# Reading the early token lists before the first expert's weights, and moving GpSimd's drains, in a fused attention and mixture-of-experts kernel

## The chip, the cores and the metric

The kernel runs on one core of one Trainium2 chip. The metric is the device time of one execution in microseconds (us). Three executions of the kernel before took 772.63, 769.27 and 769.30 us; their median is 769.3 us.

The engines are called here as the profile calls them: PE (TensorE, matrix products; PEld are its weight loads), DVE (VectorE), ACT (ScalarE), POOL (GpSimd) and SP (SyncE, which here issues only DMAs and register loads). Each works through its own instructions strictly in program order, so an instruction that waits holds up all that stands behind it on its engine.

## The reference

```python
def _attn_ref(q, k, v):                     # (8 batches, 12 heads, 448 tokens, 64)
    scores = scale * np.matmul(q, k.transpose(0, 1, 3, 2)) - np.log(S)
    attn = 1.0 / (1.0 + np.exp(-scores))    # sigmoid, no sum over a row
    return np.matmul(attn, v)

def _moe_ref(x, w_gate, w_output_gate, w1, w2):   # x: 3584 tokens x 768, 8 experts, hidden 1024
    logits = x @ w_gate
    e_idx = np.argmax(logits, axis=1)             # each token goes to one expert
    probs = softmax(logits);  gate_w = probs[arange(N), e_idx]
    eom = 1.0 / (1.0 + np.exp(-(x @ w_output_gate)))
    for e in range(E):
        h = np.maximum(x[mask] @ w1[e], 0.0)
        out[mask] = gate_w * eom[mask, e] * (h @ w2[e])
```

All of it is float32. The softmax is cut to one line above.

## The kernel before

**Attention.** 48 head pairs (8 batches x 6) are worked off in 24 groups of two, each group in 7 units, so in 168 units. The code counts units backwards: unit -168 is the first and -1 the last. One unit is `scores(u)` on PE (L823), one sigmoid of 128x896 on ACT (L825) and `values(u - 2)` on PE (L832). The scores of unit u go into one of two PSUM buffers, so they wait for the sigmoid of unit u - 2. DVE adds and transposes a head pair's result (L835 to L846); after six pairs SP writes the batch to DRAM (`x_dram`, L848). SP also loads the keys, queries and values of group g + 2 (L815, 1344 KB each) when group g runs.

**Routing.** When a batch is complete, `gates` and the generator `route` give every token its expert and its place in that expert's list. `route` has four steps, called logits, counts, places and rows, which the attention loop calls at fixed units. The last one scatters the tokens' records into the DRAM table `lst` with four indirect DMAs on POOL (L325); they write the same table, and each waits until the one before has landed. For batch 6 (the last but one) two row gathers for the second slot stand behind each scatter.

**Slots.** The experts' work is cut into slots of 256 tokens. The first three, the early slots, take only tokens of batches 0 to 5, so that they can be prepared while attention still runs; `table` (L327 on) computes on DVE which expert and which place in the list each has. To prepare a slot, SP loads its list of 256 records (`load_list`, L458), DVE transposes it and POOL spreads it into index tiles (`spread_lists`, L463), POOL gathers the rows of x with eight indirect DMAs (`gather`, L507), DVE turns them (`turn_x`, L566), and ACT and DVE split them into a rounded high part and a low rest (`split_x`). The expert's weights are loaded by SP (`load_w`, L528) and split in the same way. In a slot PE does layer 1 (L588, L589) and layer 2 (L613 to L615); while it does, DVE, ACT, POOL and SP prepare the next two slots.

**What is done during attention** is in `unit(u)` (L896): the table in units -31 to -29, the first expert's six weight rows from -28 on (L910) with their splits two units apart from -22 on (L912), the first slot's list at -21 (L914), its spreading and gather at -18, the other two early lists at -18 and their spreading at -11, the second-layer weights from -9 on, `turn_x` at -8 and `split_x` at -6, -5 and -4.

**Lists of the later slots.** The generator `side()` (L945) is stepped from the early slots' loops. It finishes the routing, computes the late table on DVE (`table_late`) and then loads the later lists in blocks of 32 rows by indirect DMAs on POOL (`load_rows`, L498); the first block is transposed on DVE right after `turn_x` of the second slot.

**Drains.** `nc.gpsimd.drain()` lets POOL go on only when its earlier work is over. The kernel before has one in the fourth slot (L661) and one at the start of each slot behind it (L643, and L703 and L741 in the slots of other shapes).

Names in the rows: `lst` the table of records, `lxs` and `lts` the spread indices, `rounded` the split weights and inputs of layer 1, `plain` their float32 raw form (and the gathered rows), `w2h`/`w2l` the split second-layer weights, `gl` the sums of layer 1, `hb` the later lists.

Of the kernel before, what the change touches and what calls it, by code (L numbers as in the profile page):

```python
# [9 lines left out]
F32 = mybir.dt.float32  # L10
# [11 lines left out]
NPAIR = H // 2  # L22
# [11 lines left out]
EARLY_BATCH = 5  # L34
ROWS_E = (EARLY_BATCH + 1) * S
EARLY = -(-(ROWS_E - E * (TS - 1)) // TS)
# [7 lines left out]
GT = 32  # L44
LGR = LATE_N // 4
KT = REST // TS
READY = (EARLY_BATCH + 1) * NPAIR + 4
OOB = 1 << 20
LROWS = (E * CAP + TS) // 128
ROUNDED = (12 * DF + 12 * TS) * 4  # L50
# [8 lines left out]
class Kernel:  # L59
# [19 lines left out]
    def memory(self):  # L79
        self.rounded = self.pool("rounded").tile([128, ROUNDED // 4], F32R, name="rounded")  # L80
        self.plain = self.pool("plain").tile([128, PLAIN // 4], F32, name="plain")
        ps = self.pool("psum", space=PSUM).tile([128, 8, 512], F32, name="ps")
        self.ps_s = [ps[:, 0:2], ps[:, 2:4]]
        self.ps_third = ps[:, 6:8]
        self.ps_o = [[ps[:, 4], ps[:, 5]], [ps[:, 6], ps[:, 7]]]
        self.mm_ps, self.mm_late = ps[:, 5], ps[:, 7]
        self.gp = ps[:, 6, 0:QT]
        self.psx = [ps[:, i].rearrange("p (d t) -> p d t", d=2) for i in (6, 7)]
        self.psh = [ps[:, i] for i in (0, 1, 2, 4, 5)]
        self.psy = [ps[:, i, 0:384] for i in (4, 5, 3, 6)]  # L90
        self.rot = {}

        c = self.carve
        w = c(0, 3, 2, 2, DF)
        self.w1s = [[w[:, d // 2, a, d % 2] for d in range(6)] for a in range(2)]
        self.w1p = [[w[:, k, a] for k in range(3)] for a in range(2)]
        self.xc = c(12 * DF * 4, 6, 2, TS)
        self.xs = [self.xc[:, :, i] for i in range(2)]

        self.w1r = c(0, 6, DF, dt=F32)  # L100
        o = 6 * DF * 4
        self.xg = c(o, 8, Q4, dt=F32)
        self.xT = c(o + XG, 6, TS, dt=F32)
        o += 2 * XG
        self.w2r = c(o, 8, DM, dt=F32)
        self.li = c(o, LROWS, 6, dt=F32)
        self.lr_e = [c(o + LROWS * 24 + i * 768, 192, dt=F32, parts=32) for i in range(2)]
        self.tmp_early = o + 4096
        self.step = c(o + 8192, B, 4, dt=F32)
        self.tokf = c(o + 8192 + 16 * B, NCH, 4, dt=F32)  # L110
# [135 lines left out]
    def init_list(self):  # L246
        nc = self.nc
        nc.gpsimd.memset(self.li, 0.0)
        for w in range(1, 4):
            nc.gpsimd.memset(self.li[:, :, w:w + 1], float(w * S))  # L250
        nc.gpsimd.memset(self.li[:, :, 4:5], float(OOB))
        nc.gpsimd.dma_start(self.lst.rearrange("(p r) w -> p r w", p=128), self.li)
        for raw in self.lr_e:
            nc.gpsimd.memset(raw, 0.0)

    def route_tiles(self):
        rp = self.pool("route")
# [197 lines left out]
        self.rot[key] = i + 1  # L455
        return tiles[i % len(tiles)]

    def load_list(self, tab, k, raw, g):  # L458
        o = self.nc.values_load(tab[0:1, 1, k:k + 1], engines=[ET.SP], min_val=0, max_val=E * CAP)
        n = raw.shape[0]  # L460
        self.nc.sync.dma_start(raw, self.lst[bass.ds(o, 32 * n), :].rearrange("(g t) w -> g (t w)", t=32))
# [177 lines left out]
    def slot(self, m, side=None, hint=None):  # L639
        tab, k = (self.tab_e, m + 1) if m + 1 < EARLY else (self.tab_l, m + 1 - EARLY)  # L640
        nx = self.load_slot(tab, k, self.lists(m + 1))
        if m > EARLY:
            self.nc.gpsimd.drain()  # L643
        self.split_w2(0)
        for f in range(8):
            if m > EARLY and f == 6:
                self.finish()
            self.layer1(f, m == 0 and f == 0)
            if f == 0 and hint is not None:
                hint()  # L650
            if f:
                self.high_low(f - 1)
            if m == 0 and f < 7:
                next(side)
            if f in (1, 3, 5):
                self.split_w2(f // 2 + 1)
            if m and side is not None and f < 7:
                next(side, None)
        self.high_low(7)
        if m == EARLY:  # L660
            self.nc.gpsimd.drain()  # L661
        self.load_w2(nx)
        self.high_w1(0)
        self.turn_x(nx)
        if m == 0:
            next(side, None)
        if m == 1:
            next(side, None)
        self.gather(self.lists(m + 2), ROWS_E if m + 2 < EARLY else NT)
        for k in range(3):  # L670
            self.split_x(nx, k)
        self.low_w1(0)
        for i, (t, n) in enumerate(((0, 0), (0, 1), (1, 0), (1, 1))):
            if i == 3 and m >= EARLY:
                self.layer2_due(self.lists(m), 1)
            else:
                ps = self.psy[(0, 1, 3)[i] if m >= EARLY else (4 * m + i) % 3]
                self.layer2(self.lists(m), t, n, self.ys[t], ps)
            if i < 2:
                self.split_w1(i + 1)  # L680
            if side is not None and i > 0:
                for _ in range(3 if m == 0 and i == 1 else 1):
                    next(side, None)
# [110 lines left out]
    def attention(self, pool, rows):  # L794
        nc = self.nc
        N = B * NPAIR
        NG = N // G
# [19 lines left out]
        def scores(u):  # L817
            g, i = divmod(u, U)
            kg = kq[g % 3]
            ps = self.ps_third if u == 2 else self.take("s", self.ps_s)  # L820
            for j, h in corners:
                e, o = (h, 384) if i == 3 else (i // 4, 128 * (i % 4) + 64 * h)
                nc.tensor.matmul(ps[half[h], j, 0:S], kg[half[j], e, 1, o:o + 64], kg[half[j], e, 0],  # L823
                                 start=True, stop=True)
            nc.scalar.activation(at[u % 4], ps[:, :, 0:S], AF.Sigmoid, bias=self.bias_s, scale=1.0 / math.sqrt(D))  # L825
# [27 lines left out]
        def routing(at):  # L853
            if routes and want[0] == at:
                want[0] = next(routes[0])
                if want[0] is None:
                    routes.pop(0)
# [17 lines left out]
        for u in range(U * NG + LAG):  # L875
            g, i = divmod(u, U)
            self.unit(u - U * NG)
            if i == 1:
                routing("places")
            if u < U * NG:  # L880
                scores(u)
            if u >= LAG:
                values(u - LAG)
            if i == 3 and g and g % 3 == 0:
                gates(g // 3 - 1)
                routing("logits")
            if i == 1 and 0 < g < NG - 2:
                load(g + 2)
            for r, name in ((0, "counts"), (3, "rows")):
                if i == r and (name != "rows" or g != NG - 2):  # L890
                    routing(name)
        self.layer1_mm(0)
        gates(B - 1)
        return routes[-1]

    def unit(self, u):  # L896
        if u == -161:
            self.row_words()
        if u == -154:
            self.init_list()  # L900
        if u == -31:
            self.tgen = self.table()
        if -31 <= u < -28:
            next(self.tgen)
        if u == -28:
            self.s0 = dict(self.lists(0), **self.slot_regs(self.tab_e, 0))
        s = self.s0 if u >= -28 else None
        for d in range(6):
            if u == -28 + d:
                self.load_w(s, self.w1, self.w1r, [d], 1)  # L910
            if u == -22 + 2 * d:
                self.split_w1_row(d)  # L912
        if u == -21:
            self.load_list(self.tab_e, 0, self.lr_e[0][0:8], 8)  # L914
        if u == -18:
            self.spread_lists(self.lr_e[0], self.lts[:, 0:1], self.lxs[:, 0:1])
            self.gather(s, ROWS_E)
            for k in range(1, EARLY):
                self.load_list(self.tab_e, k, self.lr_e[1][8 * k - 8:8 * k], 8)
        if u == -11:  # L920
            self.spread_lists(self.lr_e[1], self.lts[:, 1:EARLY], self.lxs[:, 1:EARLY])
        for k in range(4):
            if u == -9 + 2 * k:
                self.nc.vector.memset(self.w2r[0:1, 2 * k, 0:1], 0.0)
                self.load_w(s, self.w2, self.w2r, [2 * k])
        if u == -8:
            self.turn_x(s)
        for k, at in enumerate((-6, -5, -4)):
            if u == at:
                self.split_x(s, k)  # L930

    def build(self, phases="abc"):
        tc, nc = self.tc, self.nc
# [13 lines left out]
        def side():  # L947
# [12 lines left out]
            for _ in self.table_late():  # L960
                yield
            at = lambda a, n: (self.lts[:, EARLY + a:EARLY + a + n], self.lxs[:, EARLY + a:EARLY + a + n])
            self.load_rows(0)
            yield
            for i in (1, 3):
# [101 lines left out]
```

## Time and profile before

| | before |
|---|---|
| median of 3 executions | 769.3 us (769.27 to 772.63) |
| the profiled execution's own time | 772.41 us |
| its span, first to last instruction | 770.7 us |
| PE busy | 758.6 us (98%) |
| ACT busy, DVE busy | 488.5 us (63%), 486.5 us (63%) |
| POOL busy | 349.3 us (45%) |
| DMA | 145.22 MB, mean 188 GB/s |

The profile comes from one execution, the 772.41 us one. Its span leaves out 1.7 us around the first and the last instruction. An engine's busy time counts the time in which it has an instruction under way. PE's idle time is 12.1 us in all: 1.3 us at the start, some 7 us behind its last product at the end, and the rest in short waits. Attention ends, and the first slot begins, at about 273 us.

### The profile page before, as it was taken

The numbers are of one execution on the slowest core, as the hardware profiler recorded it, in microseconds if no ns is written. First come the engines' busy times: TensorE is split into PE (matmuls) and PEld (weight loads), VectorE is DVE, ScalarE is ACT, GpSimd is POOL, SyncE is SP. The second block draws the span as 40 slices with busy tenths as digits, with TensorE's granted clock in tenths as the row PEclk, the third lists the DMA queues.
The fourth block names the chain that finished last, engine by engine and source line by source line (L and its number), as shares of the span: only waits on it lengthen the run. The fifth ranks groups of instructions, "written<-read, shape, count | busy, mean of one in ns | idle before, by whom it ended". The sixth has DMA issues, their size and how long they took to land. (4 is left out here: it accounts for less than half of the span.)

```text
span 770.7 us, 15634 instructions
## 1 busy us (share of the span) xinstructions
PE 758.6 (98%) x5971; PEld 563.7 (73%) x5971; DVE 486.5 (63%) x800; ACT 488.5 (63%) x662; POOL 349.3 (45%) x472
## 2 busy tenths in 40 slices
PE   9999999999999999999999999999999999999996
PEld 4344444444444379799999989999998999889785
DVE  3343443434356668878686676768586685877887
ACT  5666666666668756566574655747465574675686
POOL 4021303122132657777785667264362724524622
PEclk9999999999999999999999999999999999999999
DMA  7353454435349450147667497611146846397692
GB/s 265 136 217 126 169 207 146 163 129 217 131 174 348 156 166 17 43 175 251 239 205 256 162 344 269 201 57 37 47 174 210 307 161 218 123 337 251 228 411 67
DMA packets 37904, 145.22 MB, mean 188 GB/s; under 512 B 5671, under 2 KB 7951, under 8 KB 33840
## 3 DMA queue, kind: packets, MB, share of 16 engines
q1 hardware_dynamic: 27984, 119.56, 43.6%
q0 software_dynamic: 9824, 24.46, 9.6%
q8 instruction: 50, 0.82, 0.4%
q14 instruction: 46, 0.38, 0.1%
HBM read 152.61 MB, written 23.05 MB: 228 GB/s over the span
## 5 line engine op out<-in xcount | busy, mean ns | idle before, releaser
L588 PE MATMUL ps<-rounded 128*128 128x512 f32 (+1 forms) x672 | 226.0, 386 | 2.0 <-DVE gl L597 1.4
L825 ACT ACTIVATE a<-ps,bias_s 128x896 f32<-128x896 f32 x168 | 169.0, 1007 | 89.6 <-PE ps L823 89.5
L510 POOL DMA_INDIRECT plain<-x_dram,lxs x122 | 180.8, 1482 | 65.2 <-issue 31.9
L589 PE MATMUL ps<-rounded 128*128 128x256 f32 (+1 forms) x672 | 183.9, 274 | 0.0
L823 PE MATMUL ps<-kqv 64*64 64x448 f32 x1344 | 157.9, 542 | 1.1 <-ACT a L825 1.1
L832 PE MATMUL ps<-a,kqv 64*64 64x448 f32 x1344 | 155.9, 536 | 0.0
L545 DVE TENSOR_TENSOR w2l<-plain,w2h 128x1536 fp32r<-128x1536 f32 x60 | 105.2, 1756 | 64.8 <-ACT w2h L544 64.8
L613 PE MATMUL ps<-w2h,h 128*128 128x384 f32 x432 | 144.8, 335 | 0.0
L588 PEld LDWEIGHTS ps<-rounded 128*128 128x128 f32 x672 | 125.9, 187 | 25.6 <-DVE gl L597 2.3
L615 PE MATMUL ps<-w2h,h 128*128 128x384 f32 x432 | 144.4, 334 | 0.0
L614 PE MATMUL ps<-w2l,h 128*128 128x384 f32 x432 | 144.4, 334 | 0.0
L589 PEld LDWEIGHTS ps<-rounded 128*128 128x128 f32 x672 | 127.3, 189 | 0.0
L832 PEld LDWEIGHTS ps<-a,kqv 64*64 64x64 f32 x1344 | 50.9, 133 | 75.4 <-issue 74.2
L551 DVE TENSOR_TENSOR rounded<-plain,rounded 128x2048 fp32r<-128x2048 f32 x46 | 103.4, 2283 | 1.9 <-ACT rounded L548 1.9
L823 PEld LDWEIGHTS ps<-kqv 64*64 64x64 f32 x1344 | 49.7, 134 | 72.7 <-issue 68.2
L596 ACT COPY gl<-ps 128x256 f32<-128x256 f32 (+1 forms) x112 | 40.3, 360 | 95.2 <-PE ps L589 89.3
L544 ACT CAST w2h<-plain 128x1536 fp32r<-128x1536 f32 x60 | 88.2, 1472 | 16.7 <-PE ps L863 5.0
L548 ACT CAST rounded<-plain 128x2048 fp32r<-128x2048 f32 x46 | 87.2, 1902 | 0.0
L613 PEld LDWEIGHTS ps<-w2h,h 128*128 128x128 f32 x432 | 81.1, 188 | 2.3 <-issue 1.8
L614 PEld LDWEIGHTS ps<-w2l,h 128*128 128x128 f32 x432 | 81.1, 188 | 0.1
L615 PEld LDWEIGHTS ps<-w2h,h 128*128 128x128 f32 x432 | 81.1, 188 | 0.0
L635 POOL DMA_INDIRECT out<-y,due x11 | 18.3, 1660 | 113.3 <-ACT gl L596 92.7
(211 smaller groups left out, 699.8 us busy)
## 6 DMA issues: line engine op xcount, KB each, us to landing
plain<-w SPq DMA_DIRECT2D x68, 768.0 KB
plain<-w SPq DMA_DIRECT2D x48, 1024.0 KB
kqv<-kqv SPq DMA_DIRECT2D x23, 1344.0 KB
x_dram<-xt SPq DMA_DIRECT2D x8, 1344.0 KB
plain<-w SPq DMA_DIRECT2D x6, 512.0 KB
plain<-x_dram,lxs POOLq DMA_INDIRECT x122, 4.1
kqv<-kqv SPq DMA_DIRECT2D x2, 448.0 KB
lst<-plain POOLq DMA_DIRECT2D x1, 726.0 KB, 8.3
```

Of the source, the lines that this page charges most:

```text
L510: self.nc.gpsimd.indirect_dma_start(out=s["xg"][:, g], out_offset=None, in_=x4, in_offset=bass.IndirectOffsetOnAxis(ap=s["lx"][:, g:g + 1] ...
L544: self.nc.scalar.copy(hi, raw)
L545: self.nc.vector.tensor_tensor(lo, raw, r32(hi), ALU.subtract)
L551: self.nc.vector.tensor_tensor(self.w1p[1][k], self.w1r[:, 2 * k:2 * k + 2], r32(self.w1p[0][k]), ALU.subtract)
L588: nc.tensor.matmul(out, wh[d][:, c], both, start=(d == 0), stop=False)
L589: nc.tensor.matmul(ps[:, 0:n], wl[d][:, c], self.xc[:, d, 0, 0:n], start=False, stop=(d == 5))
L613: nc.tensor.matmul(ps, hh[:, f, tk], wh, start=(f == 0), stop=False)
L614: nc.tensor.matmul(ps, hh[:, f, tk], wl, start=False, stop=False)
L615: nc.tensor.matmul(ps, hl[:, f, tk], wh, start=False, stop=(f == 7))
L823: nc.tensor.matmul(ps[half[h], j, 0:S], kg[half[j], e, 1, o:o + 64], kg[half[j], e, 0], start=True, stop=True)
L825: nc.scalar.activation(at[u % 4], ps[:, :, 0:S], AF.Sigmoid, bias=self.bias_s, scale=1.0 / math.sqrt(D))
L832: nc.tensor.matmul(self.ps_o[e][h][half[j], 0:S], v[half[h], 6 if i == 3 else 3 * e + c, j], a[half[h], j], start=(i in ((0, 3 if h else 4 ...
```

## The change

The three early lists are loaded together at unit -27, ahead of the first expert's weights on SP's queue, and are spread at once at -21; the second spreading at -11 is gone. The weight rows are loaded from -25 instead of -28, and split from -18 instead of -22. Batch 6's rows step is called at the first unit of the last group instead of its fourth. One drain is put at unit -40, one ahead of the first block of the later lists; the one in the fourth slot is taken out.

```diff
@@ memory, init_list
-        self.lr_e = [c(o + LROWS * 24 + i * 768, 192, dt=F32, parts=32) for i in range(2)]
+        self.lr_e = c(o + LROWS * 24, 192, dt=F32, parts=32)
...
-        for raw in self.lr_e:
-            nc.gpsimd.memset(raw, 0.0)
+        nc.gpsimd.memset(self.lr_e, 0.0)
@@ slot
         self.high_low(7)
-        if m == EARLY:
-            self.nc.gpsimd.drain()
         self.load_w2(nx)
@@ attention
             for r, name in ((0, "counts"), (3, "rows")):
-                if i == r and (name != "rows" or g != NG - 2):
+                if i == (0 if g == NG - 1 else r) and (name != "rows" or g != NG - 2):
                     routing(name)
@@ unit
     def unit(self, u):
+        if u == -40:
+            self.nc.gpsimd.drain()
...
         for d in range(6):
-            if u == -28 + d:
+            if u == -25 + d:
                 self.load_w(s, self.w1, self.w1r, [d], 1)
-            if u == -22 + 2 * d:
+            if u == -18 + 2 * d:
                 self.split_w1_row(d)
+        if u == -27:
+            for k in range(EARLY):
+                self.load_list(self.tab_e, k, self.lr_e[8 * k:8 * k + 8])
         if u == -21:
-            self.load_list(self.tab_e, 0, self.lr_e[0][0:8], 8)
-        if u == -18:
-            self.spread_lists(self.lr_e[0], self.lts[:, 0:1], self.lxs[:, 0:1])
+            self.spread_lists(self.lr_e, self.lts[:, 0:EARLY], self.lxs[:, 0:EARLY])
             self.gather(s, ROWS_E)
-            for k in range(1, EARLY):
-                self.load_list(self.tab_e, k, self.lr_e[1][8 * k - 8:8 * k], 8)
-        if u == -11:
-            self.spread_lists(self.lr_e[1], self.lts[:, 1:EARLY], self.lxs[:, 1:EARLY])
@@ side
             at = lambda a, n: (self.lts[:, EARLY + a:EARLY + a + n], self.lxs[:, EARLY + a:EARLY + a + n])
+            nc.gpsimd.drain()
             self.load_rows(0)
```

SP's queue before, from the last two weight rows (`plain<-w`) on: the first list (`plain<-lst`), then batch 6's write of x and the load of the last group's keys, queries and values. A name in brackets is a semaphore that the instruction waits for; DMASW is a DMA of POOL, DMAHW one of SP.

```order
45 L531 DMA plain<-w 128x1024 [waits DMAHW4_49]
46 L531 ISA
47 L531 DMA plain<-w 128x1024 [waits DMAHW5_49]
48 L459 TENSOR_LOAD tabe
49 L459 ISA x2
50 L461 ISA
51 L461 DMA plain<-lst 8x192 [waits DMAHW6_49,DMASW1_49,Pool_49]
52 L848 DMA x_dram<-xt_161 128x2688 [waits DMAHW7_49,DVE_49]
53 L815 DMA kqv_151<-kqv 128x2688 [waits DMAHW0_49,PE_49]
```

And of the changed kernel, from the first list on:

```order
38 L459 DMA plain<-lst 8x192 [waits DMASW1_49,Pool_49]
39 L457 TENSOR_LOAD tabe
40 L457 ISA x2
41 L459 ISA
42 L459 DMA plain<-lst 8x192 [waits DMAHW0_49]
43 L457 TENSOR_LOAD tabe
44 L457 ISA x2
45 L459 ISA
46 L459 DMA plain<-lst 8x192
47 L811 DMA kqv_150<-kqv 128x2688 [waits DMAHW3_49,PE_49]
48 L529 ISA
49 L529 DMA plain<-w 128x1024
```

The wait for the last scatter (DMASW1) stood behind all six weight rows and the load of group 22; now it stands ahead of them all, and so do the two other lists, each with a register load in front.

DVE's order before, from the last split of a weight row (128x1024) to the first split of the inputs (128x2x256), around `turn_x` (`STREAM_TRANSPOSE plain<-plain`):

```order
250 L545 TENSOR_TENSOR rounded<-plain,rounded 128x1024 [waits DMAHW5_49,Activation_49]
251 L466 STREAM_TRANSPOSE lt_102<-plain 32x192 [waits DMAHW2_49,DMAHW1_49,Pool_49]
252 L835 COPY xh<-ps 128x448 [waits PE_49]
253 L924 MEMSET plain 1x1
254 L845 TENSOR_TENSOR x_156<-xh,ps 128x448 [waits DVE_49,PE_49]
255 L846 STREAM_TRANSPOSE xt_162<-x_156 128x14x32 [waits DVE_49]
256 L570 STREAM_TRANSPOSE plain<-plain 128x8x6x32 [waits DMASW4_49,DMASW5_49,DMASW3_49,DMASW6_49,DMASW2_49,DMASW7_49,DMASW1_49,DMASW0_49]
257 L924 MEMSET plain 1x1
258 L545 TENSOR_TENSOR rounded<-plain,rounded 128x2x256 [waits Activation_49]
```

And of the changed kernel, the same stretch:

```order
249 L543 TENSOR_TENSOR rounded<-plain,rounded 128x1024 [waits DMAHW7_49,Activation_49]
250 L831 COPY xh<-ps 128x448 [waits PE_49]
251 L919 MEMSET plain 1x1
252 L841 TENSOR_TENSOR x_156<-xh,ps 128x448 [waits DVE_49,PE_49]
253 L842 STREAM_TRANSPOSE xt_162<-x_156 128x14x32 [waits DVE_49]
254 L543 TENSOR_TENSOR rounded<-plain,rounded 128x1024 [waits DMAHW0_49,Activation_49]
255 L568 STREAM_TRANSPOSE plain<-plain 128x8x6x32 [waits DMASW4_49,DMASW5_49,DMASW3_49,DMASW6_49,DMASW2_49,DMASW7_49,DMASW1_49,DMASW0_49]
256 L919 MEMSET plain 1x1
257 L318 RECIPROCAL den<-den 128x4 [waits Pool_49]
258 L543 TENSOR_TENSOR rounded<-plain,rounded 128x2x256 [waits Activation_49]
```

The last weight row's split now stands directly ahead of `turn_x`, the second transposition of lists is gone, and the reciprocal that opens batch 6's rows step stands directly behind it. PE's order is the same in both kernels.

## Rows read from the trace of the kernel before

**Rows 1.** The page's first part: the span; busy time, share, instructions.
```profile
span 770.7 us, 15634 instructions
PE 758.6 (98%) x5971; PEld 563.7 (73%) x5971; DVE 486.5 (63%) x800; ACT 488.5 (63%) x662; POOL 349.3 (45%) x472
```

**Rows 2.** PE's waits over the span: us in total, times, longest.
```profile
PE ps L588 <- DVE gl L597: 1.4, 3, 0.8
```

**Rows 3.** Timeline of PE: start us, us, instruction [idle before <-releaser].
```profile
246.03 0.93 PE L823 MATMUL ps<-kqv 64*64 64x448 f32 x8
...
260.01 0.93 PE L823 MATMUL ps<-kqv 64*64 64x448 f32 x8
...
265.85 0.98 PE L823 MATMUL ps<-kqv 64*64 64x448 f32 x8 [1.15 <-ACT a L825]
...
346.38 0.28 PE L589 MATMUL ps<-rounded 128*128 128x256 f32 x1
```

**Rows 4.** Timeline of ACT, the first split of the inputs.
```profile
264.27 0.62 ACT L544 CAST rounded<-plain 128x512 fp32r<-128x512 f32 x1 [2.19 <-DVE plain L924]
```

**Rows 5.** Timeline of DVE, end of attention and the second slot.
```profile
259.39 0.65 DVE L846 STREAM_TRANSPOSE xt<-x 128x448 f32<-128x448 f32 x1
262.45 1.78 DVE L570 STREAM_TRANSPOSE plain<-plain 128x1536 f32<-128x1536 f32 x1 [2.42 <-DMA plain<-x_dram,lxs]
...
297.33 1.78 DVE L570 STREAM_TRANSPOSE plain<-plain 128x1536 f32<-128x1536 f32 x1 [2.25 <-DMA plain<-x_dram,lxs]
...
333.67 0.52 DVE L466 STREAM_TRANSPOSE lt<-hb 32x192 f32<-32x192 f32 x1 [0.55 <-DMA hb<-lst,gl]
...
335.90 6.68 DVE L551 TENSOR_TENSOR rounded<-plain,rounded 128x2048 fp32r<-128x2048 f32 x3
```

**Rows 6.** DVE's instructions by form, 240 to 262 us: busy us, mean ns.
```profile
L545 DVE TENSOR_TENSOR rounded<-plain,rounded 128x1024 fp32r<-128x1024 f32 x5 | 6.1, 1212 | 2.3 <-ACT rounded L544 2.3
```

**Rows 7.** Timeline of POOL.
```profile
218.06 0.25 POOL L308 TENSOR_TENSOR pos<-pc,off 128x32 f32<-128x32 f32 x1 [16.57 <-ACT pc L306]
...
228.71 0.92 POOL L325 DMA_INDIRECT lst<-meta,posi  x1 [1.40 <-DMA lst<-meta,posi]
233.48 0.91 POOL L325 DMA_INDIRECT lst<-meta,posi  x1 [3.85 <-DMA lst<-meta,posi]
...
247.76 1.95 POOL L510 DMA_INDIRECT plain<-x_dram,lxs  x1 [0.15 <-POOL lts L473]
...
258.19 0.95 POOL L510 DMA_INDIRECT plain<-x_dram,lxs  x1 [0.30 <-issue]
...
268.93 0.21 POOL L322 TENSOR_TENSOR meta<-eom,den 128x4 f32<-128x4 f32 x1 [2.65 <-DVE plain L924]
...
330.00 1.05 POOL L635 DMA_INDIRECT out<-y,lts  x1 [2.87 <-issue]
...
334.92 8.40 POOL L499 DMA_INDIRECT hb<-lst,gl  x1 [0.30 <-issue]
...
409.99 1.74 POOL L496 COPY gl<-lts 32x10 f32<-32x10 f32 x1
```

**Rows 8.** POOL's sequencer at line 661: durations ns min/median/max, start us.
```profile
L661 POOLq DRAIN  x1: 9871/9871/9871, 409.1 to 409.1; - x1
```

**Rows 9.** Timeline of SP's DMA issues.
```profile
229.22 1.04 SPq L531 DMA_DIRECT2D plain<-w  x2
...
239.40 0.35 SPq L461 DMA_DIRECT2D plain<-lst  x1
...
245.52 2.98 SPq L461 DMA_DIRECT2D plain<-lst  x2
```

**Rows 10.** SP's register loads at line 504, 220 to 240 us: ns min/median/max.
```profile
L504 SPq TENSOR_LOAD <-tabe x2: 273/373/473, 227.5 to 228.3; - x2
```

**Rows 11.** Stretches: us, busy times, then PE clock, DMA share, GB/s.
```profile
229.00:230.00 1.00, 1.00 (x16) 0.46 (x12) 0.36 (x1) 0.96 (x1) 0.63 (x1) 1.00 0.03 8
231.10:241.10 10.00, 10.00 (x112) 4.03 (x108) 4.77 (x7) 8.20 (x10) 0.91 (x1) 1.00 0.98 371
```

More of the change, by code (lines that the diff above doesn't have):

```diff
@@ L46 @@
 KT = REST // TS
-READY = (EARLY_BATCH + 1) * NPAIR + 4
 OOB = 1 << 20
@@ L456, in take, with load_list @@
         return tiles[i % len(tiles)]
-    def load_list(self, tab, k, raw, g):
+    def load_list(self, tab, k, raw):
         o = self.nc.values_load(tab[0:1, 1, k:k + 1], engines=[ET.SP], min_val=0, max_val=E * CAP)
```

## The prediction, made before the changed kernel was run

> **What bounds the kernel now.** I read the page's first part, then PE's waits, then the timelines around them. PE is busy for 758.6 of 770.7 us [rows 1], and the change leaves PE's instructions and their order as they are. So the time can fall only by idle time of PE, and rises only where the change makes PE wait. In the middle of the kernel PE waits in two places that the change can reach:
>
> - once for a sigmoid, 1.15 us just before 265.85 [rows 3];
> - three times for DVE's sums of layer 1, 1.4 us together, 0.8 the longest [rows 2]; all three lie in the second slot.
>
> Both go back to a late gather of rows. At the first place DVE is through with its earlier work at 260.04 (259.39 + 0.65), but waits until 262.45 for the first slot's gather before it can turn x; it is done at 264.23 [rows 5]. ACT waits 2.19 us for that with its next split, and the sigmoid that PE needs stands behind this split [rows 4]. At the second place `turn_x` waits 2.25 us, until 297.33, for the second slot's gather [rows 5], and DVE is pressed from there up to the three waits. Take both away and 1.15 + 1.4, some 2.5 us, is all there is to win; 0.5% of 769.3 us, about the least that a measurement of this kernel can tell from no change, is 3.85 us.
>
> **The lists.** Before, the first list was issued at 239.40 [rows 9], because the last scatter, issued at 233.48, landed only 5.8 us later [rows 7, 9], while the weight rows filled the DMA engines (371 GB/s, 98% of them busy, from 231.1 on [rows 11]). Now nothing stands ahead of the scatters. With that a scatter takes 0.92 us to issue and 1.40 more to land, as the rows at 228.71 show [rows 7]; so I put the fourth at 231.1 and its landing at 233.5, where SP issues list 0. A register load and its checks took about 0.86 us here (two between 227.5 and 229.22 [rows 9, 10]), an issue 0.35 [rows 9]: list 1 at 234.7, list 2 at 235.9, the keys of group 22 at 236.3, the first weight row at about 236.9 instead of 229.22. Estimate: list 2 has landed by 238.3. DVE's transposition waits a little over 1 us for it, with nothing urgent behind it. POOL's 12 copies take 2.3 us and the eight gathers 11.4 (247.76 to 259.14 before [rows 7]): 241.1 to 252.5. The last one landed 3.3 us after its issue before (262.45 against 259.14); with 3.5 more, which the full DMA engines cost the scatter (5.8 against 2.3), it is there at 259.3.
>
> What moves back in SP's queue are three list loads, one load of keys and six weight rows, and behind them batch 6's write of x and the last group's keys. The weight rows: a first transfer needs about 1 us to flow (issued 229.22, 8 GB/s up to 230.0 [rows 9, 11]); keys and first row are 1344 + 512 KB, 5.1 us at 371 GB/s; so the first row is there at 242.4. ACT splits it in front of the sigmoid of unit -18, which PE needs at 246.03 [rows 3]; split and sigmoid take 2.0 us, so 244.0 would do. Margin 1.6 us, cost 0. Each further row takes 1.4 us to flow and has 3 us. The last group's keys: 1344 x 3 + 512 x 6 KB is 7.27 MB, 19.6 us, and the gathers' 0.8 MB 2.1 us more, all beginning at 237.3: there at 259.0, wanted at 260.01 [rows 3]. Margin 1.0 us, cost 0; what comes later than that, PE pays in full. The splits on ACT are as many as before, one in every second unit.
>
> **First gain.** DVE now does the last weight row's split (1.21 us, the mean [rows 6]) directly ahead of `turn_x`: 260.04 + 1.2 + 1.78 = 263.0 instead of 264.23. PE went on 1.62 us after that end, at 265.85, having stood since 264.70 (265.85 - 1.15) [rows 3]; now it can go on at 264.65. I leave 0.1 us of the 1.15: **1.05 us won**, by DVE's own load and no longer by the gather.
>
> **Second gain.** POOL loses 12 copies (2.4 us), is through with the first gather 6.6 us sooner, and batch 6's rows step stands right behind `turn_x`: its first instruction at about 263.3 instead of 268.93 [rows 7], 5.6 us sooner. The four scatters and the second slot's eight gathers follow in line. The wait of 2.25 us plus the 1.05 that PE now comes earlier, 3.3 us, has to be made up, and 5.6 covers it if the scatters' landings don't eat more than 2.3. I count all of it: **1.4 us won**.
>
> **The drains.** No row shows a drain at these two places. The one in the fourth slot was over at 418.9 (409.1 + 9.87 [rows 8]), 7.2 us after POOL's last work at 411.73 [rows 7], with 23 of POOL's transfers made since the load that took 8.40 us [rows 7] (about 0.9 is usual); I read both as clearing up behind old transfers. That drain held the gather of a later slot, and PE did not wait anywhere near; taking it out brings nothing, and the next drain, with some 36 transfers to clear, is hidden as the old one was.
>
> At unit -40 POOL has 22 transfers behind it, is idle from 201.5 and gets its next input at 218.06, after 16.57 us [rows 7]. Between 0 and 8.4 us disappear in that; queued behind is only batch 5's route, which waits for ACT anyway.
>
> The drain ahead of the later lists is dearer. Queued behind it are the five list loads, their copies and the fourth slot's gathers, and DVE waits for the first list. POOL is free there at 331.05 (330.00 + 1.05 [rows 7]), 5.6 us sooner now: 325.4. Bounds: 0 us, and 38 transfers at 7.2/23 each, 11.9 us. I take the nearest row, 7.2: the load is issued at 332.6, lands 2.3 us later (before: issued at 331.35, 0.3 behind the last output, transposed at 333.67 [rows 5]) at 334.9. DVE comes there at 333.1 - 2.4 = 330.7 and waits 4.2 us. It has slack: its last weight split ended at 342.58 (335.90 + 6.68 [rows 5]), and PE wants it at 346.38 [rows 3], 3.8 us. **Cost 0.4 us**; with 11.9 it is 5.1 us, with 0 nothing. What goes in return is the 8.40 us load, which no longer meets a full queue, but that one PE never waited for.
>
> **Sum.** -1.05 - 1.4 + 0.4 = -2.0 us (rounded): 772.4 becomes 770.4 us for the profiled execution. The median, 769.3, lies 3.1 us below that execution, and no row says where; I take the same difference from it: 767.3 us. If the faster executions lack the two waits, the gain is nothing.
>
> **The rivals.**
>
> - *Hidden anyway, or not there* (769.3 us). The gather is no longer late, but DVE's added split, landings of batch 6's scatters (four of them, under the second-layer weights' traffic) or a drain give it all back; or the waits belong to the profiled execution only. For it: 2.5 us is small beside the 3.1 us between the executions. Against: the chain from the gather to PE is plain in the rows.
> - *Slower: the weights come late.* ACT works in order; a first weight row after 244.0 holds sigmoids and so PE, us for us. If the scatter lands 5.8 us after its issue as before and each list costs 2.6 us (the two of 245.52 together 2.98, less 0.35 [rows 9]), list 0 goes at 236.9, the keys at 242.5, and the first row is there at 248.6: 4.6 us too late. The first wait is then not met (1.15), and the second gain comes or not: 771.4 to 772.8 us. For it: those are the durations that the trace has. Against: both were seen with the DMA engines full.
> - *Slower: the drain before the later lists costs 11.9 us*: 5.1 lost, 2.4 won, 772.0 us; it turns the sign once PE loses more than the 2.4, at some 9 us.
> - *Slower: POOL's issues are held by DVE.* The weight rows' splits now lie beside the first gathers. With every gather at 1.95 us, the longest that the rows show [rows 7], and 0.30 between two, eight take 18 us, are out at 259.1 and land, under full DMA engines, at 265.9, 3.4 us later than before: 772.7 us. It decides from a landing after 262.45 on. Against: beside three such splits the eight gathers took 11.4 us. The Trainium skill ("SBUF — State Buffer", sections "SBUF: two separate sides" and "A bandwidth-pool intuition that's wrong (but worth ruling out)") speaks for this rival: a DVE instruction with two SBUF inputs can lock GpSimd out for its whole length, and a DMA issued by GpSimd took some 3.1 us beside a DVE copy instead of 0.62. By that figure, as an estimate, eight gathers would last 27 us and PE would lose about 9 us. The trace shows 1.95 us for the worst of the eight, so it agrees in kind and not in size.
>
> **Chances.** Forecast, 766.5 to 768.4 us: 0.53. No gain, 768.4 to 770.5: 0.25. Weights or last keys late: 0.10. Drain: 0.07. POOL held: 0.05. More than 3.85 us won needs more than the two waits hold, 0.05; more than 3.85 us lost takes a third of the last three cases, and more than one of them at once, 0.08; within 0.5%: 0.87. The range of 765.6 to 772.4 us holds the first two cases, the mild half of the others, and leaves under 2 in 10.
>
> **What would show it.** Right: list loads on SP at 233 to 236; no wait of PE at 264 of over 0.3 us; `turn_x` of the second slot without a wait; PE's waits for layer 1's sums below 0.3 us; the first drain over before 218; the 8.40 us load gone. Wrong: a sigmoid waiting for a weight row's split around 242 to 246, a PE wait for keys near 260, DVE waiting more than 4 us for the first later list, or a wait of PE at 340 to 350.

## The result, and the profile after

| | before | after |
|---|---|---|
| median, 4 executions each | 769.28 us (769.12 to 772.63) | 774.0 us (773.77 to 775.49) |
| ratio | | 1.0062 (95% interval 1.0039 to 1.0084) |
| the profiled execution's own time | 772.41 us | 774.12 us |
| its span | 770.7 us | 772.4 us |

The change makes the kernel 4.7 us slower; 767.3 was predicted. The two profiled executions differ by 1.7 us only. Where the other 3.0 us are is half of the answer, and stands with the experiments.

PE's waits after, over the span (us in total, times, longest):

```profile
PE ps L819 <- ACT a L821: 1.7, 1, 1.7
PE ps L869 <- DVE rounded L865: 1.3, 1, 1.3
PE ps L819 <- DMA kqv<-kqv: 1.0, 1, 1.0
...
PE ps L587 <- DVE rounded L549: 0.4, 1, 0.4
```

The waits of [rows 2, 3] are gone, for layer 1's sums as well as the one before 265.85. Three others are there instead: 1.7, 1.0 and 0.4 us (the 1.3 at L869 is in the kernel before too). The timelines (start us, us, instruction [idle before <-releaser]; lines of the changed kernel are 2 to 5 lower) lead to their cause. PE and ACT first:

```profile
248.45 0.98 PE L819 MATMUL ps<-kqv 64*64 64x448 f32 x8 [1.68 <-ACT a L821]
...
263.67 0.98 PE L819 MATMUL ps<-kqv 64*64 64x448 f32 x8 [1.01 <-DMA kqv<-kqv]
...
346.97 0.38 PE L587 MATMUL ps<-rounded 128*128 128x256 f32 x1 [0.38 <-DVE rounded L549]
```

```profile
246.44 1.04 ACT L542 CAST rounded<-plain 128x1024 fp32r<-128x1024 f32 x1 [3.90 <-DMA plain<-w]
247.39 1.90 ACT L821 ACTIVATE a<-ps,bias_s 128x896 f32<-128x896 f32 x2
```

ACT stands for 3.90 us ahead of the first weight row's split, with two sigmoids queued behind it; PE needs the first of them. Why the row is late stands on SP's queue and on POOL, where the fourth scatter is the row at 231.88:

```profile
235.78 3.43 SPq L459 DMA_DIRECT2D plain<-lst  x3
239.31 0.37 SPq L811 DMA_DIRECT2D kqv<-kqv  x1
240.04 3.71 SPq L529 DMA_DIRECT2D plain<-w  x6
243.85 0.40 SPq L844 DMA_DIRECT2D x_dram<-xt  x1
245.19 0.34 SPq L811 DMA_DIRECT2D kqv<-kqv  x1
```

```profile
231.88 0.91 POOL L323 DMA_INDIRECT lst<-meta,posi  x1 [1.74 <-DMA lst<-meta,posi]
...
335.60 0.90 POOL L497 DMA_INDIRECT hb<-lst,gl  x1 [4.53 <-issue]
...
339.16 8.48 POOL L497 DMA_INDIRECT hb<-lst,gl  x1 [0.30 <-issue]
```

SP waits for the scatter until 235.8, and only then do keys and weight rows leave, 10.8 us later than the 229.22 of [rows 9]. The last group's keys are at the end of that line: issued 245.19, wanted at 262.66 (263.67 - 1.01), there 1.01 us later. The second POOL row is the drain ahead of the later lists (POOL's output before it ended at 331.07); the third shows that the long load of [rows 7] came all the same. DVE's rows say what the gathers and that drain did:

```profile
263.68 1.77 DVE L568 STREAM_TRANSPOSE plain<-plain 128x1536 f32<-128x1536 f32 x1
...
297.37 1.77 DVE L568 STREAM_TRANSPOSE plain<-plain 128x1536 f32<-128x1536 f32 x1
...
338.00 0.53 DVE L464 STREAM_TRANSPOSE wg<-hb 32x192 f32<-32x192 f32 x1 [4.84 <-DMA hb<-lst,gl]
```

Neither of these two `turn_x` waits any more [rows 5]; the transposition of the first later list does, for 4.84 us where it was 0.55.

### The profile page after: what moved, and what is told of

Its sections match the earlier page's. It is cut to its first block, busy times and chain, and to the rows that moved or that the text cites. A ratio compares the mean times of both kernels' runs of the same rounds, so it can differ in the third digit from the quotient of the medians.

```text
span 772.4 us, 15622 instructions
## 1 busy us (share of the span) xinstructions
PE 759.5 (98%) x5971; PEld 564.9 (73%) x5971; DVE 485.3 (63%) x799; ACT 488.8 (63%) x662; POOL 353.3 (46%) x459
## 5 line engine op out<-in xcount | busy, mean ns | idle before, releaser
L633 POOL DMA_INDIRECT out<-y,due x11 | 20.8, 1888 | 115.4 <-ACT gl L594 93.1
```

## The experiments

Each ratio is against the kernel before on its own chip. On two of the chips (those of lists_only, drains_only, keys_first, before_again, and of first_drain_only, keys_first_old_drains, before_third, one_more_transfer) the kernel before has a median of 778.8 to 779.4 us, on the others 769.3 to 769.6. "PE behind by" is the start of one and the same matmul in two traces, each counted from its first matmul, one less the other; before_fourth, after_again and weights_first share a chip, and the first traces of before and after come from another measurement.

**Which half of the change costs the time.** Lists alone, the drains put back:

```
-        if u == -40:  self.nc.gpsimd.drain()
-            nc.gpsimd.drain()          # ahead of load_rows(0)
+        if m == EARLY: self.nc.gpsimd.drain()
```

> The changed kernel with its drains put back as before: no drain at u = -40 nor ahead of load_rows(0), the drain of slot 4 again. Theory 1 (the lists hold SP: keys of group 22 and six weight rows stand behind three list loads that wait for the fourth scatter): the two new waits of PE, 1.7 for a near 248 and 1.0 for kqv near 263, stay, and the time is 773.0 to 774.0, at most 0.7 below the changed kernel's 773.9. Theory 2 (the drains are the loss, through POOL's later work and the transfers behind it): 769 to 770.

Drains alone, the same three places in the kernel before:

> The kernel before with the drains alone changed: one at u = -40, one ahead of load_rows(0), none in slot 4; lists and weights as before. Theory 1 (the lists are the loss): 769.3 to 770.0, a drain ahead of load_rows(0) giving PE a wait of about 0.6 near 346. Theory 2 (the drains are the loss): 773 to 774.

Measured: 1.0060 (1.0037 to 1.0083) for the lists, 1.0022 (1.0001 to 1.0043) for the drains. So by the times the lists are most of the loss and the drains a smaller part, whose interval only just leaves out 1. But the two waits that were expected in the trace of lists_only are not there. PE's waits in it:

```profile
PE ps L821 <- issue: 1.4, 3, 0.5
...
PE ps L821 <- ACT rounded L542: 0.4, 1, 0.4
PE ps L821 <- ACT a L823: 0.3, 1, 0.3
```

PE stops again and again between 245 and 254 without a releaser that the profile shows ("issue"); it is 7.4 us behind before_again at 250, and 1.0 at 290, since before_again has such stops near 283. What makes them on this chip is not shown. How the lists cost PE is therefore read from after and after_again, which have no such stops. With the drains alone DVE waited 5.16 us for the first later list and PE 0.67 at 350.96, `<-DVE rounded L551`.

**The two drains apart.** The changed kernel without the drain ahead of `load_rows(0)`:

> The changed kernel without the drain ahead of load_rows(0); the drain at u = -40 stays. If that second drain costs what the traces show near 346 (PE 0.5 to 0.7 later against the kernel before from there on), this kernel's PE has no step there and is 0.6 us faster than the changed kernel: 0.5% above the kernel before where the changed kernel is 0.6% above. If it costs nothing, the step of 0.5 to 0.7 near 346 stays; if the first drain is the dear one, the time stays at 0.6% above with the step gone.

Measured: 1.0048 (1.0021 to 1.0075). In its trace DVE waits 0.61 us for that list and PE's lag doesn't change between 342 and 346, where it grows by 0.66 in the changed kernel's. So the second drain holds DVE and costs PE those 0.66 us; the first drain, at unit -40, has no wait beside it in any trace. The times alone don't separate 1.0048 from 1.0062. The second drain costs more one slot on. `turn_x` of the fourth slot, in after and in first_drain_only:

```profile
368.91 1.78 DVE L568 STREAM_TRANSPOSE plain<-plain 128x1536 f32<-128x1536 f32 x1 [4.86 <-DMA out<-y,lts]
```

```profile
371.38 1.78 DVE L568 STREAM_TRANSPOSE plain<-plain 128x1536 f32<-128x1536 f32 x1
```

In all four traces with the second drain it waits 4.7 to 5.7 us, for work of POOL that stood behind the drain, and PE loses 0.3 to 1.5 us between 355 and 405; in first_drain_only it doesn't wait and PE loses nothing there. One trace without that drain, gathers_later, has such a wait too (5.14) and loses 0.7.

**What stands behind the lists.** The list loads one unit later, which lets the keys of group 22 out ahead of them:

```
-        if u == -27:
+        if u == -26:
             for k in range(EARLY): self.load_list(...)
```

> The changed kernel with the three list loads one unit later (u = -26 for -27), which puts the load of the keys of group 22 ahead of them on SP's queue; nothing else moves on any engine. Theory 1 (what is queued behind the lists' wait is the loss): 1344 KB leave the queue behind the lists, 3.3 us at 400 GB/s, so both new waits of PE (1.7 and 1.0 us in the trace, 1.9 and 1.25 against the kernel before) go or fall under 0.3, and the time is 770.6 to 771.2. Theory 2 (the drains): 773.5 to 774. A third (the transfer of the keys holds the fourth scatter back, as in the kernel before, and the lists come that much later): 772 to 773.

Measured: 1.0008 (0.9979 to 1.0037) with both drains, against 1.0060 for lists_only on the same chip. The same with the drains as before:

> The three list loads early, but behind the keys of group 22 (u = -26), and the drains as in the kernel before (slot 4 alone). It has the change's two gains (turn_x of slot 0 sooner, POOL sooner in slot 0) and neither of its losses. Theory A (PE's waits at 264.7 and in slot 1, 1.15 and 1.36 in the trace before, are in most executions): 2.0 to 3.0 us, 0.25 to 0.4%, faster than the kernel before. Theory B (they are in the profiled execution of 772.4 and not in those of 769.3): the same time as the kernel before, within 0.15%.

Measured: 0.9987 (0.9954 to 1.0019), which fits both theories. Its SP and ACT rows show the third case of the first expectation too:

```profile
229.88 0.33 SPq L813 DMA_DIRECT2D kqv<-kqv  x1
238.07 3.40 SPq L459 DMA_DIRECT2D plain<-lst  x3
241.83 3.82 SPq L529 DMA_DIRECT2D plain<-w  x6
```

```profile
245.53 1.04 ACT L542 CAST rounded<-plain 128x1024 fp32r<-128x1024 f32 x1 [3.30 <-DMA plain<-w]
```

Beside the keys' transfer the fourth scatter, issued at 232.26, lets SP go on 5.8 us later (3.9 in after), the lists leave 2.3 us later, and ACT still waits for the row; but the queue behind is 1344 KB shorter, and PE waits neither for the row's sigmoid near 247 nor for keys (its 1.84 us for a later sigmoid, at 259.11, has its like in before_third, 1.59). A new wait has come: DVE's transposition of the lists holds a head pair's sum behind it until 243.70, and PE waits 1.03 us for that at 244.38 (2.06 in keys_first). Then the weight rows too ahead of the lists, all three lists together, with the drains as before:

```
-            if u == -25 + d:            # load of weight row d
+            if u == -28 + d:
-            if u == -18 + 2 * d:        # its split
+            if u == -22 + 2 * d:
-        if u == -27:                    # the three list loads
+        if u == -22:
-        if u == -21:                    # spread, gather
+        if u == -18:
```

> One set of list loads for all three early slots as in the change, but behind the six weight rows on SP's queue (loads of the rows at u = -28 to -23 and their splits as in the kernel before, lists at u = -22, one spread and the gathers at u = -18); drains as before. If what stands behind the lists' wait is the whole loss, no wait of PE near 246 or 260 over 0.3 is left, and the time is the kernel before's (Theory B: its own waits at 264.7 and in slot 1 are not in most executions) or 1 to 2.5 us below it (Theory A). If the single late spread itself costs something (lists 1 and 2 ahead of the x store and the last keys), a wait for kqv or for DVE appears between 250 and 265 and the time is 0.2 to 0.5% above.

Measured: 1.0000 (0.9981 to 1.0019), 769.7 us. PE's waits:

```profile
PE ps L871 <- DVE rounded L867: 1.3, 1, 1.3
PE ps L586 <- PEq L1004: 0.7, 1, 0.7
PE ps L760 <- PEq L1009: 0.7, 1, 0.7
```

The lists still come in one set, with one spread, and batch 6's rows step still stands at the first unit: only SP's order, the units that hang on it and the drains are the old ones, and with them the whole loss is gone. None of the waits that were to be won is there. Yet the time is the kernel before's and not 2.5 us below it: so the gain had not been there to win.

**Were the two gains ever there?** The kernel before three times more, for its trace:

> The kernel before, instruction for instruction, for a second trace of it: its profiled execution took 772.4 us where its median is 769.3, so the trace that the prediction was read from may hold about 3 us that most executions don't have. Theory A (the trace before was typical in its waits, and the 3 us lie in something spread out or outside): median 769.3, and the second trace shows the same waits of PE again, 1.15 near 264.7 and 0.81, 0.21, 0.34 in slot 1. Theory B (the waits themselves come and go): a second profiled execution near 769.3 lacks 1 to 3 us of these waits, and what the change could gain there was never to be had in most executions.

> The kernel before once more, for a third trace. Theory A: PE's waits for a near 264.7 (1.15) and for gl in slot 1 (0.81, 0.21, 0.34) are there again. Theory B: in an execution at the kernel's median they are gone, and PE's idle time is some 9 us of the span where the first trace had 12.1.

> The kernel before, a trace more, beside after_again. Theory B: PE's wait for a near 264.7 and the 0.81 in slot 1 are absent here too, so of four traces one has them. Theory A: both are there.

And the changed kernel a second time:

> The changed kernel once more, for a second trace beside the kernel before on the same chip. Theory 1: PE falls behind the kernel before by 3 us or more between 243 and 250 (ACT held by the first weight row), gets back 2.5 or less by 330, loses 0.6 near 346; 0.5 to 0.7% slower. A theory by which the loss was of the first measurement alone: within 0.2%.

before_again and before_third ran at 778.6 and 778.4 us (1.0007, 0.9995). The wait before 265.85 and the longest of slot 1, 0.8, are not there, but they don't decide, because PE is late there for other reasons. A few units before, PE waits for a sigmoid already:

```profile
259.18 0.98 PE L823 MATMUL ps<-kqv 64*64 64x448 f32 x8 [1.95 <-ACT a L825]
```

```profile
260.19 0.98 PE L823 MATMUL ps<-kqv 64*64 64x448 f32 x8 [1.59 <-ACT a L825]
```

By 260 it is 5.4 and 1.6 us behind before_fourth, and from 265 to 281 it loses 5.0 and 5.6 more, with stops like those in lists_only. before_fourth is the clean one, 769.51 us, at the median. Its first lines and all of PE's waits:

```profile
span 767.8 us, 15634 instructions
...
PE 757.7 (99%) x5971; PEld 564.0 (73%) x5971; DVE 486.3 (63%) x800; ACT 489.1 (64%) x662; POOL 350.3 (46%) x472
```

```profile
PE ps L873 <- DVE rounded L869: 1.3, 1, 1.3
PE ps L588 <- PEq L1009: 0.7, 1, 0.7
PE ps L762 <- PEq L1014: 0.7, 1, 0.7
PE ps L823 <- DMA kqv<-kqv: 0.2, 1, 0.2
```

Against the first trace, PE is 1.38 us sooner from 265 on and 2.13 more by 326 (1.08, 0.50, 0.55), 3.5 in all, at the places of the four waits that I had counted as gains (2.5 by their rows). With 0.2 lost at the start that is 3.3 us at 748, and the spans differ by 2.9 (770.7 and 767.8). The times say how often: of the 34 executions of the kernel before that were measured beside after, after_again and gathers_later, 29 took 768.5 to 770.2 us and 5 took 772.2 to 775.2, none between. So Theory B holds, by one clean trace and these times. Against before_fourth, PE is behind by (us, at the time in before_fourth):

| | 243 | 247 | 261 | 342 | 346 | 405 | 748 |
|---|---|---|---|---|---|---|---|
| after | 0.37 | 2.28 | 3.52 | 3.58 | 4.24 | 4.69 | 4.71 |
| after_again | -0.24 | 0.92 | 2.28 | 2.41 | 2.96 | 4.48 | 4.29 |
| weights_first | -0.25 | -0.25 | -0.25 | -0.22 | -0.22 | -0.22 | -0.19 |

The granted clock is 1.00 from 230 to 410 in all of these traces, so it has no part in the steps. after_again measured 1.0056 (1.0038 to 1.0075) and shows the same steps: weight row 1.16, keys 1.36, second drain 0.55, and 1.5 us in the slot behind it (0.4 in the first trace), where `turn_x` waits 5.67 us (4.86). PE's rows at the first two:

```profile
247.09 0.98 PE L819 MATMUL ps<-kqv 64*64 64x448 f32 x8 [0.92 <-ACT a L821]
```

```profile
262.43 0.98 PE L819 MATMUL ps<-kqv 64*64 64x448 f32 x8 [1.13 <-DMA kqv<-kqv]
```

**Why one execution had waits that others lack.** The kernel before with two of the four spreads of slot 0's list done twice on POOL:

```
-        for i in range(4):
+        for i in (0, 1, 2, 3, 0, 1):    # slot 0's list alone
```

> The kernel before with six more instructions on POOL and nothing else: two of the four list spreads of slot 0 are done twice (the same values written again), which puts its eight gathers 0.95 us later. In the trace of 772.4 us the gathers stand 1.1 us later than in that of 769.5, by a first gather of 1.95 us for 1.01 and a list 0.3 us later, and PE then has waits of 1.4, 1.1, 0.5 and 0.55 us more. If those waits hang on that one microsecond of POOL: this kernel has them in most executions, PE waits 1.1 to 1.4 near 264.7 and for gl in slot 1, and it takes 772 to 773, 0.35 to 0.45% more than the kernel before. If they come from something else in that execution: within 0.1% of the kernel before. On a chip where PE is held for some 7 us by other waits between 245 and 290 (the kernel before then takes 777 to 779) it should show nothing by either.

Measured: 1.0053 (1.0039 to 1.0067), 773.65 us, 1 us beyond the 772 to 773 expected. POOL's first gather and DVE's and PE's rows:

```profile
247.67 1.94 POOL L510 DMA_INDIRECT plain<-x_dram,lxs  x1 [0.15 <-POOL lts L473]
```

```profile
262.35 1.78 DVE L570 STREAM_TRANSPOSE plain<-plain 128x1536 f32<-128x1536 f32 x1 [2.37 <-DMA plain<-x_dram,lxs]
```

```profile
265.74 0.98 PE L823 MATMUL ps<-kqv 64*64 64x448 f32 x8 [1.10 <-ACT a L825]
```

The picture of [rows 3, 5, 7] comes back: a first gather of 1.94, `turn_x` held 2.37, PE 1.10. By 323 PE is 2.5 us further behind before_fourth than at 260. Another 2.8 come later, 2.0 of them between 441 and 443, which the first trace did not have. So the kernel sits at an edge here: the first gather begins only 0.23 us later than in before_fourth (247.44, the last section has the row), takes 0.93 us longer, and the first wait is there.

**The long load.** One transfer more on POOL, at the very start:

```
-        nc.gpsimd.dma_start(lst, self.li)
+        for p in (slice(0, 64), slice(64, 128)):
+            nc.gpsimd.dma_start(lst[p], self.li[p])
```

> The kernel before, with init_list's write to the list table (POOL's second transfer) in two halves of 64 partitions: every later transfer of POOL has an ordinal one higher, and no drain is moved. In all six traces so far one issue of POOL takes 8.4 to 10.1 us, the fourth hb load, which is POOL's 64th transfer since the start, with a drain five transfers ahead of it or none. Theory 'what is outstanding' (the prediction's: a drain resets it): as in the kernel before, the fourth hb load long. Theory 'the count' (the 64th transfer since the start, whatever it is): the third hb load takes 8.4 us, the fourth about 0.9. Time: within 0.2% of the kernel before by either.

Measured: 0.9994 (0.9957 to 1.0031), and neither theory: no load is long.

```profile
334.38 1.62 POOL L501 DMA_INDIRECT hb<-lst,gl  x1 [0.30 <-issue]
336.31 1.02 POOL L501 DMA_INDIRECT hb<-lst,gl  x1 [0.30 <-DVE gl L599]
337.63 0.86 POOL L501 DMA_INDIRECT hb<-lst,gl  x1 [0.30 <-issue]
```

In after_again it was the third hb load, POOL's 63rd transfer, with 9.61 us. What sets it stays open. That 8 us of POOL go and the time stays says, within that interval, that the load costs the kernel before nothing; behind the second drain, where POOL's work comes later, that was not tried.

## Why the prediction was wrong

1. **The base.** The step that failed first is "The median, 769.3, lies 3.1 us below that execution, and no row says where; I take the same difference from it". The 3.1 us lay at the very waits counted as gains: PE loses 3.5 us there against before_fourth, and without them the kernel takes 769.5, with them 772.4. The prediction even says "If the faster executions lack the two waits, the gain is nothing", and gives that case 0.25. In an execution at the median, -2.45 is 0.
2. **The weight rows** ("there at 242.4", "Margin 1.6 us, cost 0"). The first row was there at 246.44. The 4.0 us between are four short terms: the fourth scatter issued 0.8 later (231.88 for 231.1), 1.5 more until SP could go on (3.9 for 2.4; I took the usual landing, and this one took longer with hardly any other transfers), 0.7 more for three list loads (3.5 for 2.8), 1.0 more for keys and row (7.1 for 6.1). PE paid 1.9 and 1.2 us in two executions. The margin was smaller than the error of a sum of four estimates, and all four erred to one side.
3. **The last keys** ("there at 259.0", "Margin 1.0 us, cost 0"). There at 263.7, 1.2 to 1.4 us too late, paid in full as said. Both late transfers have one cause; keys_first takes it from the keys, weights_first from both.
4. **First and second gain.** The first gather did begin sooner, at 243.04 for 247.44 in before_fourth, both `turn_x` run without a wait, and no wait for layer 1's sums is left. But before_fourth has none of these waits either, so their absence is no gain (point 1). POOL's rows step began at 265.70 instead of 263.3; in before_fourth it began at 266.86.
5. **The drains.** The first was over by 205.9 (199.0 + 6.9), well before 218, cost 0, as forecast. The second let the load go 4.53 us behind POOL's last output, where 7.2 was put; DVE waited 4.84 us (forecast 4.2), and PE paid 0.55 to 0.66 (0.4). That this comes so near is luck: POOL was free at 331.07 and not at 325.4, and DVE came 2.5 us later than put, which all but cancel against the shorter drain. The fourth slot's gathers, named as queued behind the drain, had no price; through them PE paid 0.4 and 1.5 us more. "The 8.40 us load gone" was wrong: it came as the fourth transfer behind the drain.
6. **The rivals.** "The weights come late" was the right mechanism, with chance 0.10 for it and the keys together; its 771.4 to 772.8 stood on the wrong base. "Not there" was right at the same time. I had treated them as exclusive. POOL held by DVE: the eight gathers took 11.0 us (243.04 to 254.03), not 18, so that rival fell here.

From a base of 769.5 the steps add up: 1.9 + 1.2 + 0.7, 0.4 in the slot behind the drain and 0.4 at the start make 4.6, the distance between 767.8 and 772.4; the 0.4 at the start has no cause on record. The forecast missed by 6.7 us: 2.45 of gain that was not there, 1.9 and 1.2 put at 0, 1.1 for the drain put at 0.4, and the 0.4 at the start.

## What to carry to other kernels

When the profiled execution is longer than the median by about as much as the waits one hopes to remove, those waits may be that excess: take a second trace before pricing them. A load that waits for a late result belongs behind the loads that could already go, because an in-order queue passes its wait on to all of them. And a margin that is the difference of two long sums is worth no more than their error.

## What was not expected of the hardware

- **A gather that begins beside a DVE instruction.** In the first trace of before, the 1.95 us gather of [rows 7] began 0.14 us behind the start of a weight row's split on DVE; in gathers_later, 0.17. In before_fourth it began 0.31 us ahead of the split, and took 1.01. DVE's row of the first trace, and both rows of before_fourth:

```profile
247.62 1.21 DVE L545 TENSOR_TENSOR rounded<-plain,rounded 128x1024 fp32r<-128x1024 f32 x1
```

```profile
247.75 1.23 DVE L545 TENSOR_TENSOR rounded<-plain,rounded 128x1024 fp32r<-128x1024 f32 x1 [0.37 <-ACT rounded L544]
```

```profile
247.44 1.01 POOL L510 DMA_INDIRECT plain<-x_dram,lxs  x1 [0.15 <-POOL lts L473]
```

  The long ones end 0.89 us behind the split, about a whole gather. Over all 14 traces, between 240 and 262 us, 35 gathers begin inside such a split and end 0.81 to 0.95 us behind it; 28 begin ahead of one that starts while they run, and took 0.95 to 1.02. The Trainium skill ("SBUF — State Buffer", section "SBUF: two separate sides") has the one of the two that starts first, a DVE instruction with two SBUF inputs or a GpSimd one that reads SBUF, hold a shared port for its whole length and block the other. The rows agree for the gather that starts inside the split. Of a split that starts inside a gather they show no block: those 28 splits took 1.18 to 1.25 us, the one in before_fourth 1.23 for the 1.21 of the first trace.
- **A register load on SP** took 0.26 us ahead of list 0 before, and 1.06 and 1.81 us ahead of lists 1 and 2, with the DMA engines full; after, on idle DMA engines, 0.47 to 0.48.
- **One slow hb load** of 8.4 to 10.1 us in 13 of 14 traces, the fourth of the five in 12 of them and the third in one, behind a drain or not, and gone with one transfer more at the start.
